# An FFT convolution beside an FFN: other slots for the steps of the convolution and for the last stage of each tile

## The chip, the cores and the metric

The kernel runs on one core of a Trainium2 chip. A core has a matrix engine (TensorE, PE in the profile, with its weight loads listed as PEld), a vector engine (VectorE, DVE), an activation engine (ScalarE, ACT), a general engine (GpSimd, POOL) and a queue engine that mostly issues transfers (SyncE, SP). Each engine works through its own instructions in order and waits on semaphores that the others raise. The metric is the time of one execution on the device in microseconds (us). Time before: a median of 2299.88 us in three runs (2294.12 to 2300.57).

## The reference: what is computed

```python
batch, seq, d_model = (4, 12544, 128)
...
h_filt = (np.maximum(pos_emb @ w1, 0.0) @ w2) * window
u = x * v
L = 2 * S
Uf = np.fft.rfft(u, n=L, axis=1)
Hf = np.fft.rfft(h_filt, n=L, axis=0)
y = np.fft.irfft(Uf * Hf[None, :, :], n=L, axis=1)[:, :S, :]
x = (x * y).reshape(B * S, D)
...
h = np.maximum(np.maximum(x @ w1, x @ w2), x @ w3)
return h @ w_out
```

A long convolution along the sequence, by Fourier transforms, gated by `x`, for four batches of 12,544 positions and 128 channels. Its result goes through a feed-forward network (FFN) whose 768 hidden values are the maximum of three products, all in float32.

## The kernel before

**Stages.** The convolution of batch 0 and the spectrum of the filter are made first. Then the FFN of batch 0 runs with the convolution of batch 1 beside it, the FFN of batch 1 beside the convolution of batch 2, and so on. The FFN of the last batch runs alone, with another arrangement. In this text "batch b" of a schedule is the batch whose convolution is laid out, so it lies beside the FFN of batch b - 1.

**Slots.** The FFN of one batch has `NT` = 32 tiles of 392 positions, and each tile has `NF` = 6 slots, one for each 128 hidden values: 192 slots to a batch. The main loop (from L1100) issues in each slot: `up` (two products into the three `hps` buffers, taken in turn; ScalarE's relu of the first, VectorE's maximum with the second), perhaps sums of the next tile (`t_sums`), `down` of the slot two before (into `ops`, with the extra product `lin` at a tile's first), perhaps the next tile's last stage `t_last`, and then, by `run`, the steps of the convolution that are due in this slot. As each engine runs in order, this order of issue is the order of the work on each engine.

**The last stage of a tile.** `t_load` brings `zt` (what the convolution left in `zd`) and `xT`. `t_sums` makes two sums of 90x512 values, on GpSimd in the first part of a batch and on VectorE later. `t_last` multiplies them by `f4p` into one of two `cps` buffers, and VectorE multiplies the result by `xT` into `gt` (L717), the FFN's input. The `plan` has for each tile the slots of its two sums and of `t_last` (0 to 5).

**The convolution's steps.** They come in two parts.

- *Units*: `NU` = 32 of them. A unit's chain is `u_load` (two loads, SyncE's queue), `u_mul` (VectorE), `u_planes` (GpSimd splits into 16-bit planes), `u_dma` (a transposing transfer, SyncE's queue), `u_join` (ScalarE and VectorE), and `u_first` (32 matmul records into a `cps` buffer, then one copy on ScalarE and two operations on VectorE that write `spec`).
- *Pairs*: `NK` + `LATE` = 48 steps `x`, two to a start slot, called a double here. Each does a `g_quarter` into a `cps` buffer (a first half for pair `x`, a second for pair `x - 3`), and `g_fold` one slot (for odd `x` two slots) later. `w_load`, `q_load` and `h_load` bring its operands over SyncE's queue; `q_swap`, `q_re`, `q_im`, `q_unfold` multiply by the filter's spectrum on ScalarE, VectorE and GpSimd; `g_store` writes `zd` from GpSimd's queue.

`t_last`, `u_first` and `g_quarter` take the two `cps` buffers in turn, one each:

```python
pairs = itertools.cycle([cps.tile([P, 1024], FP32, name=f"cps{i}") for i in range(2)])
```

**The planner.** `conv_steps` (L577) gives each step its slot. `per_pair` is the number of slots per pair; units are 0.6 of it apart. `done` units (6 in batch 1, none later) have been prepared before. `s0` is the slot of the first double and `start(x)` the slot of step `x`. `emptiest` puts sums and VectorE's part of the pairs into the slot with the least planned load. The position `last` of `t_last` in its tile is the first of 3, 4, 2 that is not the slot after a double's start. The slots of one batch's steps begin at 0 and end by 182.

Of the kernel before, what the change touches and what calls it, by code (L numbers as in the profile page):

```python
# [28 lines left out]
LATE = 3  # L29
# [62 lines left out]
def kernel(  # L92
# [16 lines left out]
    NG, _, _, B, NB = x.shape  # L109
# [3 lines left out]
    NF = DFF // P  # L113
    NK = N1 // 2
# [37 lines left out]
    def halves_mm(out, lhsT, rhs, start, stop):  # L152


        for h in range(2):
            nc.tensor.matmul(out[64 * h:64 * h + 64], lhsT[:, 64 * h:64 * h + 64], rhs,  # L156
                             start=start, stop=stop, skip_group_check=True)
# [183 lines left out]
    NU = NG  # L341
# [235 lines left out]
    def conv_steps(b, done):  # L577


        out = []  # L580

        def at(slot, late, fn, *args):
            out.append((slot, late, len(out), fn, args))

        for u in range(4, done):
            at(2 * u - 7, 1, u_first, u)
        per_pair = 170 / (NK + LATE + 0.6 * (NU - done))
        for u in range(done, NU):  # L590
            s = (u - done) * 0.6 * per_pair + 9
            at(max(0, int(s) - 9), 0, u_load, b, u)
            at(int(s) - 6, 0, u_mul, u)
            at(int(s) - 5, 0, u_planes, u)
            at(int(s) - 4, 0, u_dma, u)
            at(int(s), 0, u_join, u)
            at(int(s + 1), 1, u_first, u)
        s0 = int((NU - done - 1) * 0.6 * per_pair + 9) + 6

        def start(x):  # L600
            return s0 + int(x // 2 * 2 * per_pair)

        load = [0.6] * (NT * NF)
        for x in range(NK + LATE):
            s = start(x)
            load[s] -= 1.2
            load[s + 1 + x % 2] += 1.4

        def emptiest(among, cost):
            s = min(among, key=lambda i: load[i])  # L610
            load[s] += cost
            return s

        plan = []
        folds = {start(x) + 1 for x in range(NK + LATE)}
        for i in range(NT - 1):
            s = i * NF
            last = min((3, 4, 2), key=lambda k: s + k in folds)
            load[s + last] += 0.6
            if s <= s0:  # L620
                plan.append((0, 0, last))
                continue
            a = emptiest(range(s, s + 2), 0.7) - s
            plan.append((a, emptiest(range(s + a, s + max(a + 1, last - 1)), 0.7) - s, last))
        plan.append((3, 3, 4))

        for x in range(NK + LATE):
            s, odd = start(x), x % 2
            g, z = x if x < NK else None, x - LATE if x >= LATE else None
            at(s, 1, g_quarter, g, z)  # L630
            at(s + 1 + odd, 0, g_fold, g, z)
            at(s - 4, 0, w_load, x)
            if z is not None:
                at(s + 3 + odd, 0, g_store, b, z)
            if g is None:
                continue
            if g % 2 == 0:
                at(s - 4, 0, q_load, g, min(2, NK - g))
                at(s - 1, 0, h_load, g, min(2, NK - g))
            first = s + 2 + 2 * odd  # L640
            at(first, 0, q_swap, g, 0)
            at(first + 1, 0, q_swap, g, 64)
            last = start(x + LATE) - 1
            a = emptiest(range(first + 1, min(first + 3, last - 1) + 1), 0.7)
            at(a, 0, q_re, g)
            a = emptiest(range(a, min(first + 4, last - 1) + 1), 0.7)
            at(a, 0, q_im, g)
            two = sorted(emptiest(range(a + 1, last + 1), 0.55) for _ in range(2))
            for q in range(2):
                at(two[q], 0, q_unfold, g, q)  # L650
        slots = {}
        for s, _, _, fn, args in sorted(out, key=lambda r: r[:3]):
            slots.setdefault(s, []).append((fn, args))
        return slots, plan, s0


    N = 4 * NB
    NT = P // 4
    zts, xTs, gs, pos_, obs = ({} for _ in range(5))

    def t_load(b, i):
        zt = hp.tile([N1, 2, 512], FP32, tag="zt", name="zt", bufs=2)
        for c in range(2):
            if b == 0:
                nc.sync.dma_start(
                    zt[NK * c:NK * c + NK],
                    zd[b].rearrange("(g a) c t f -> g a c t f", a=2)[
                        :, :, c, 2 * i:2 * i + 2, :].rearrange("g a t f -> g a (t f)"))
                continue
            q, j = divmod(i, NT // 2)  # L670
            for a in range(2):
                nc.sync.dma_start(
                    zt[NK * c:NK * c + NK, a].rearrange("g (t f) -> g t f", t=2),
                    zd[b].rearrange("(g a) c t q f -> g a c t q f", a=2)[
                        :, a, c ^ (a & q), 2 * j:2 * j + 2, q, :])
        zts[b, i] = zt[:, 0], zt[:, 1]
        if i % 2:
            return
        xT = hp.tile([D, 2, 4, NB], FP32, tag="xT", name="xT", bufs=2)
        for c in range(GC):  # L680
            nc.sync.dma_start(xT[c * NG:(c + 1) * NG].rearrange("d i p n -> d (i p) n"),
                              x[:, 4 * i:4 * i + 8, c, b, :])
        xTs[b, i], xTs[b, i + 1] = xT[:, 0], xT[:, 1]
# [3 lines left out]
    def t_sums(i, eng=nc.gpsimd, parts=(0, 1)):  # L687
        z0, z1 = zts[i]
        if 0 in parts:
            evens_[i] = hp.tile([N1, 512], FP32, tag="even", name="even", bufs=2)  # L690
        even = evens_[i]
        for a, (out, op) in enumerate(((even[:], ALU.add), (z1, ALU.subtract))):
            if a not in parts:
                continue
            if i[0] == 0 or i[1] < NT // 2:
                eng.tensor_tensor(out=out, in0=z0, in1=z1, op=op)
            else:
                nc.vector.scalar_tensor_tensor(out=out, in0=z1, scalar=sign_t[:, 0:1], in1=z0,
                                               op0=ALU.mult, op1=op)
        if 1 in parts:  # L700
            zts[i] = evens_.pop(i)[:], z1

    def t_last(i):
# [7 lines left out]
        for s in range(4):  # L711
            for a in range(2):
                halves_mm(y[:, s, a * h:a * h + h], zt[a][:, s * D:(s + 1) * D],
                          f4p[:, i[0] > 0 and i[1] >= NT // 2, a, :], s == 0 and a == 0, True)
        y = y.rearrange("d p (a m) -> d p m a", a=2)
# [124 lines left out]
    def run(steps):  # L840
        for fn, args in steps:
            fn(*args)
# [58 lines left out]
    for f in range(0, FO, 4):  # L901
        quad([hs[:, f + i] for i in range(4)], (f1h[:, 0], f1h[:, 1]), specH[:, :, :, f:f + 4])
        u, k = divmod(f // 4, 4)
# [11 lines left out]
    for u in range(0, NU, 2):  # L915
        t = uts.pop(u)
        for v in range(2):
            if u + 4 < NU:
                u_mul(u + 4 + v)
            at = 4 * (u + v)  # L920
# [94 lines left out]
    EARLY = 6  # L1015
# [80 lines left out]

    tiles = [(b, i) for b in range(B) for i in range(NT)]
    LAST = (B - 1) * NT
    late = []
    for n, (b, i) in enumerate(tiles[:LAST]):  # L1100
        if i == 0:
            beside, plan, pairs_from = conv_steps(b + 1, EARLY if b == 0 else 0)
        if n == 0:
            t_load(*tiles[0])
            t_load(*tiles[1])
            t_sums(tiles[0], nc.vector)
            u_first(2)
            t_last(tiles[0])
            u_first(3)
        for f in range(NF):  # L1110

            if i < NT - 2:
                if f == 0:
                    t_load(*tiles[n + 2])
            elif i == NT - 1 and f < 2 and n + 1 + f < len(tiles):
                t_load(*tiles[n + 1 + f])
            turn_ = i == NT - 1
            if f == 4 and n + 1 == LAST:
                t_sums(tiles[n + 2], nc.vector)
            h = up((b, i), f)  # L1120
            for a in range(2):
                if f == plan[i][a]:
                    t_sums(tiles[n + 1],
                           nc.vector if turn_ or i * NF > pairs_from else nc.gpsimd, (a,))
            late.append(((b, i), f, h))
            if len(late) > 2:
                down(*late.pop(0))
            if f == plan[i][2]:
                t_last(tiles[n + 1])
            if f == 5 and n + 1 == LAST:  # L1130
                t_last(tiles[n + 2])
            s = i * NF + f
            run(beside.pop(s, ()))
            if s == NT * NF - 1:
                assert not beside, sorted(beside)
    first = up((B - 1, 0), 0)
    for l in late:
        down(*l)
# [23 lines left out]
    step, b = 0, B - 1  # L1162
    for i in range(0, NT, 2):
        h = {}
        X, Y = banks if i % 4 == 0 else banks[::-1]
        for j, (name, f) in enumerate(ORDER):
            n = int(name[1]) - 1
# [64 lines left out]
```

## Time and profile before

| what | value |
|---|---|
| the profiled execution's own time | 2298.59 us |
| its span, first to last instruction | 2296.8 us |
| granted TensorE clock, mean | 0.997 |
| median of three runs | 2299.88 us |
| `hps` matmuls (`up`) | 6144 records, 1148.4 us busy |
| `ops` matmuls by `hid` (`down`) | 2304 records, 479.2 us busy |
| `u_first` matmuls (L413) | 3008 records, 134.2 us busy |
| quarter matmuls (L467, L477) | 4320 records, 87.7 and 83.0 us busy |
| `gt` (L717) beside a convolution | 98 operations, 564 ns each |
| unfold (L523) | 270 operations, 594 ns each |
| `ut` loads to landing, median | 4.1 and 4.4 us |
| `sq` loads to landing, median | 7.1 us |

A row of a timeline has the start in us from the span's start, the length in us, the engine (with a q where it is the engine's queue of transfers), the line, the operation, its output and inputs by the program's names, the shape, the number of merged instructions, and in brackets the idle time before it with what ended that. Matmuls are pipelined and their ends are modelled, so the length of a slot is best read from start to start: from the first `hps` row of one slot to that of the next. A row of waits says who waited for whom, for how long in total, how often, and the longest.

### The profile page before, as it was taken

Reading aid. Unit: us, or ns where it says so; the run is one execution under the profiler, and the core shown is the slowest. Engines: PE = TensorE matmul, PEld = TensorE weight load, DVE = VectorE, ACT = ScalarE, POOL = GpSimd, SP = SyncE. Lnnn points to the kernel's source line nnn. Section 1 sums busy time; section 2 is a strip of 40 time slices with the busy share of each in tenths; the row PEclk is TensorE's granted clock in tenths of the full one; section 3 lists DMA queues with packets and bytes.
Section 4 is the critical chain, followed back from the end, with each engine's and each line's share of the span. In section 5 each row is a group of like instructions: output and inputs, shape, how many; then the busy total and the mean of one; then the engine's idle time right before and its main releaser. Section 6 shows DMA issues by size and latency. Waiting matters only on the chain.

```text
span 2296.8 us, 68538 instructions
## 1 busy us (share of the span) xinstructions
PE 2262.9 (99%) x27855; PEld 1375.4 (60%) x27855; DVE 1555.3 (68%) x2848; ACT 1174.7 (51%) x2124; POOL 876.0 (38%) x1093
## 2 busy tenths in 40 slices
PE   8999989999999999999999999999999999999998
PEld 7988866655555546655555546655555556666665
DVE  5588957667878747758887847757887854445443
ACT  2688834456666534446666624446666622222222
POOL 2044423323333234413333324323333326666666
PEclk9999999999999999999999999999999999999999
DMA  7779969799999669969999759969999832222221
GB/s 186 182 235 272 297 159 184 148 212 240 238 232 232 170 142 190 185 149 259 241 238 249 199 126 200 185 147 233 248 253 246 211 90 55 55 64 66 63 55 22
DMA packets 473269, 411.03 MB, mean 179 GB/s; under 512 B 327865, under 2 KB 374426, under 8 KB 472954
## 3 DMA queue, kind: packets, MB, share of 16 engines
q1 hardware_dynamic: 445954, 329.48, 63.9%
q0 software_dynamic: 26288, 75.47, 11.1%
q8 instruction: 219, 3.59, 0.7%
q10 hardware_dynamic: 712, 1.70, 0.3%
q14 instruction: 96, 0.79, 0.1%
HBM read 262.84 MB, written 84.67 MB: 151 GB/s over the span
## 4 chain that ended last, share of the span: by engine, by line
PE 87%; DMA 6%; DVE 3%; SPq 1%; issue 1%; ACT 1%; POOL 0%; DVEq 0%; POOLq 0%; ACTq 0%
PE hps L156 40%; PE ops L156 16%; PE ops L790 6%; PE cps L413 5%; PE cps L156 3%; PE ps L156 3%; PE ps L165 3%; PE cps L467 3%; PE cps L477 2%; DMA ht<-hd 2%; PE sps L1000 2%; PE gps L982 1%; DMA wt<-wq_const 1%; PE last L156 1%; DMA hd<-ht 1%; DMA sq<-spec 1%
## 5 line engine op out<-in xcount | busy, mean ns | idle before, releaser
L156 PE MATMUL hps<-gt,w_sb 128*64 128x392 f32 x6144 | 1148.4, 494 | 0.0
L727 ACT ACTIVATE hid<-hps 128x392 f32<-128x392 f32 x768 | 383.9, 500 | 727.6 <-PE hps L156 712.8
L156 PEld LDWEIGHTS hps<-gt,w_sb 128*64 128x64 f32 x6144 | 427.9, 137 | 423.3 <-issue 395.2
L730 DVE TENSOR_TENSOR hid<-hid,hps 128x392 f32<-128x392 f32 x768 | 428.4, 558 | 342.9 <-PE hps L156 338.0
L156 PE MATMUL ops<-hid,wo_sb 128*64 128x392 f32 x2304 | 479.2, 492 | 0.0
L519 POOL TENSOR_TENSOR cb<-cb,xs 128x512 f32<-128x512 f32 x135 | 174.5, 1292 | 474.3 <-DVE xs L516 347.7
L156 PEld LDWEIGHTS ops<-hid,wo_sb 128*64 128x64 f32 x2304 | 170.2, 137 | 209.0 <-issue 209.0
L424 DVE TENSOR_TENSOR spec<-cps,high 128x360 f32<-128x360 f32 x188 | 141.3, 793 | 127.3 <-ACT high L422 126.3
L492 DVE TENSOR_TENSOR cb<-cps,eo 128x512 f32<-128x512 f32 (+1 forms) x288 | 175.3, 650 | 72.0 <-ACT eo L489 72.0
L745 POOL DMA_DIRECT2D out_dram<-ot x96 | 74.9, 781 | 366.8 <-ACT ot L743 312.6
L507 ACT ACTIVATE xs<-cb 32x512 f32<-32x512 f32 x270 | 169.5, 628 | 19.6 <-DVE cb L492 10.9
L508 ACT COPY xs<-cb 32x512 f32<-32x512 f32 x270 | 166.3, 616 | 3.1
L422 ACT COPY high<-cps 128x360 f32<-128x360 f32 x94 | 75.1, 799 | 162.1 <-PE cps L413 131.6
L523 DVE TENSOR_TENSOR xs<-cb 128x256 f32<-128x256 f32 x270 | 147.9, 594 | 10.9 <-POOL cb L519 10.9
L413 PEld LDWEIGHTS cps<-f1q,uT 98*64 98x64 f32 x3008 | 130.7, 137 | 32.6 <-issue 32.0
L413 PE MATMUL cps<-f1q,uT 98*64 98x90 f32 x3008 | 134.2, 241 | 2.2 <-DVE spec L424 1.5
L382 POOL COPY planes<-ut 128x784 uint16<-128x784 uint16 x90 | 75.7, 841 | 119.4 <-DVE ut L361 117.4
L500 POOL DMA_DIRECT2D zd<-cb x135 | 92.7, 689 | 50.8 <-DVE cb L492 47.6
L156 PEld LDWEIGHTS cps<-f4p,even 90*64 90x64 f32 x1568 | 89.9, 138 | 35.2 <-issue 33.2
L814 POOL DMA_DIRECT2D out_dram<-o x128 | 77.4, 610 | 51.8 <-DVE o L807 49.6
L156 PE MATMUL cps<-f4p,zt 90*64 90x49 f32 x1568 | 97.2, 222 | 0.0
L467 PE MATMUL cps<-sq,wt 64*64 64x128 f32 x2160 | 87.7, 277 | 8.8 <-DVE gt L717 6.9
(134 smaller groups left out, 3149.1 us busy)
## 6 DMA issues: line engine op xcount, KB each, us to landing
ht<-hd SPq DMA_DIRECT2D x264, 256.0 KB, 6.9
wt<-wq_const SPq DMA_DIRECT2D x144, 256.0 KB, 6.3
zd<-cb POOLq DMA_DIRECT2D x135, 256.0 KB, 6.3
zt<-zd SPq DMA_DIRECT2D x384, 90.0 KB, 3.0
sq<-spec SPq DMA_DIRECT2D x264, 128.0 KB, 7.1
ut<-in_xr_dram SPq DMA_DIRECT2D x128, 196.0 KB, 4.1
ut<-in_vr_dram SPq DMA_DIRECT2D x128, 196.0 KB, 4.4
xT<-in_x_dram SPq DMA_DIRECT2D x256, 98.0 KB, 3.7
```

The lines of the kernel that those rows point to most:

```text
L156: nc.tensor.matmul(out[64 * h:64 * h + 64], lhsT[:, 64 * h:64 * h + 64], rhs, start=start, stop=stop, skip_group_check=True)
L413: nc.tensor.matmul(ps[64 * c:64 * c + 64, 256 * i + h * N1:256 * i + (h + 1) * N1], t[:, 2 * ((at + i) % 8) + h].rearrange("n r t -> n (r ...
L424: nc.vector.tensor_tensor(out=spec[:, :, a, at:at + n], in0=v[:, 1], in1=high, op=op)
L467: nc.tensor.matmul(ps[64 * a:64 * a + 64, at:at + D], w[64 * r:64 * r + 64, k, a, :], t[64 * r:64 * r + 64, k, a, :], start=(k == 0), stop ...
L492: nc.vector.tensor_tensor(out=cb[:, a, lo:hi], in0=ps[:, lo:hi], in1=eo[:, lo:hi], op=op)
L507: nc.scalar.mul(xs[at:at + 32], xt[at + 32:at + 64], -1.0)
L508: nc.scalar.copy(xs[at + 32:at + 64], xt[at:at + 32])
L519: nc.gpsimd.tensor_tensor(out=xts[g], in0=xts[g], in1=xs[:], op=ALU.add)
L523: nc.vector.tensor_tensor(out=ab[:, q], in0=y[:, 0], in1=y[:, 1], op=(ALU.subtract, ALU.add)[q])
L727: nc.scalar.activation(h[:], pa[:, 0:N], Relu)
L730: nc.vector.tensor_tensor(out=h[:], in0=h[:], in1=pb[:, 0:N], op=ALU.max)
L790: nc.tensor.matmul(ps[64 * c:64 * c + 64, 0:H2], w, rhs[:, H2 * c:H2 * c + H2], start=start, stop=True, skip_group_check=True)
```

## The change

The planner gets other numbers. The last slot that a double may start in is set to about 177 by `END`; the first unit's join moves from slot 9 to slot 6 in batch 1 and to slot 1 in batches 2 and 3, where the loads and the next steps of the first units get negative slots. These are issued in the last slots of the FFN of the batch ahead; for that the steps of all batches are gathered in one table before the loop. The slots per double are 5.44 (from 5.35) in batch 1 and 5.29 (from 5.06) in batches 2 and 3, and `s0` is 52 (from 55) and 56 (from 62). `last` now avoids a double's start slot first of all, and the slot after it next.

```diff
         for u in range(4, done):
-            at(2 * u - 7, 1, u_first, u)
-        per_pair = 170 / (NK + LATE + 0.6 * (NU - done))
+            at(2 * (u - 4), 1, u_first, u)
+        lead, low = (1, -NT * NF) if b > 1 else (6, 0)
+        share = UNIT * (NU - done - 1)
+        per_pair = (END - lead - 6) / (share + (NK + LATE) // 2 * 2 - 2)
         for u in range(done, NU):
-            s = (u - done) * 0.6 * per_pair + 9
-            at(max(0, int(s) - 9), 0, u_load, b, u)
-            at(int(s) - 6, 0, u_mul, u)
-            at(int(s) - 5, 0, u_planes, u)
-            at(int(s) - 4, 0, u_dma, u)
+            s = (u - done) * UNIT * per_pair + lead
+            load_ = max(low, int(s) - 9)
+            at(load_, 0, u_load, b, u)
+            mul = max(load_ + 2, int(s) - 6)
+            at(mul, 0, u_mul, u)
+            at(max(mul, int(s) - 5), 0, u_planes, u)
+            at(max(mul + 1, int(s) - 4), 0, u_dma, u)
             at(int(s), 0, u_join, u)
             at(int(s + 1), 1, u_first, u)
-        s0 = int((NU - done - 1) * 0.6 * per_pair + 9) + 6
+        s0 = int(share * per_pair + lead) + 6
...
-        folds = {start(x) + 1 for x in range(NK + LATE)}
+        busy = {start(x): 2 for x in range(NK + LATE)}
+        for x in range(NK + LATE):
+            busy.setdefault(start(x) + 1, 1)
         for i in range(NT - 1):
             s = i * NF
-            last = min((3, 4, 2), key=lambda k: s + k in folds)
+            last = min((3, 4, 2), key=lambda k: busy.get(s + k, 0))
...
+    UNIT, END = 0.6, 178
...
+    besides, plans = {}, []
+    for b in range(1, B):
+        slots, *rest = conv_steps(b, EARLY if b == 1 else 0)
+        plans.append(rest)
+        for s, steps in slots.items():
+            besides.setdefault((b - 1) * NT * NF + s, []).extend(steps)
...
-            s = i * NF + f
-            run(beside.pop(s, ()))
+            run(besides.pop(n * NF + f, ()))
```

No step is added or taken away: every engine executes the same instructions, in another order.

More of the change, by code (lines that the diff above doesn't have):

```diff
@@ L1099 @@
     late = []
+    besides, plans = {}, []
[4 more added lines that the diff above has]
+            besides.setdefault((b - 1) * NT * NF + s, []).extend(steps)
     for n, (b, i) in enumerate(tiles[:LAST]):
         if i == 0:
-            beside, plan, pairs_from = conv_steps(b + 1, EARLY if b == 0 else 0)
+            plan, pairs_from = plans[b]
         if n == 0:
@@ L1131 @@
                 t_last(tiles[n + 2])
-            s = i * NF + f
-            run(beside.pop(s, ()))
-            if s == NT * NF - 1:
-                assert not beside, sorted(beside)
+            run(besides.pop(n * NF + f, ()))
+    assert not besides, sorted(besides)
     first = up((B - 1, 0), 0)
```

## The prediction, made before the changed kernel was run

> **What bounds the kernel.** I read the page's first part, then TensorE's waits over the span, then TensorE's timeline around each of those waits, then VectorE's and GpSimd's timelines beside it.
>
> ```profile
> PE 2262.9 (99%) x27855; PEld 1375.4 (60%) x27855; DVE 1555.3 (68%) x2848; ACT 1174.7 (51%) x2124; POOL 876.0 (38%) x1093
> ```
>
> ```profile
> PE cps L467 <- DVE gt L717: 6.9, 8, 0.9
> ...
> PE cps L413 <- DVE spec L424: 1.5, 1, 1.5
> ...
> PE cps L467 <- DMA sq<-spec: 1.1, 2, 0.7
> ...
> PE cps L477 <- DVE gt L717: 0.8, 1, 0.8
> ```
>
> TensorE (PE) is busy 99% of the span. A wait line reads: us in total, times, longest. The largest wait is one thing: a quarter stage (L467, once L477) waits nine times for VectorE (DVE) to finish `gt`, the product that ends a tile's last stage (`t_last`). So TensorE's work sets the end, and a change that only moves work can win what TensorE loses in waits and nothing else. The 2,296.8 us span holds about 1,559 us of FFN slots with a convolution beside them (313.5 to 1872.9).
>
> The length of a slot is the step from one `up` to the next in TensorE's timeline. Undisturbed slots repeat to 0.02 us: bare 1.98; plus 0.66 with `lin`; plus 0.91 with `t_last`; plus 1.24 with a unit's `u_first`; plus 2.05 with a double, two `g_quarter` in one slot (0.05 of it in the slot after). Prices do not depend on the neighbours: `t_last` and a unit in one slot make 4.15, the sum. **So the order of work is free on TensorE unless something waits.** In the unit stage nothing waits:
>
> ```profile
> 850.00:990.00 140.00, 140.00 (x1794) 87.66 (x1792) 97.10 (x172) 65.38 (x113) 55.91 (x78) 1.00 1.04 180
> ```
>
> The columns are the window, its length, busy time of PE, PEld, DVE, ACT, POOL, the clock, DMA share, GB/s. TensorE is busy 140.00 of 140 us at clock 1.00, and every slot there has its plain price. Units wider apart win nothing here.
>
> **What the change removes.** From the old formulas I list where a double starts in the slot of a `t_last`: batch 1 slots 81, 87, 129, 135, 177; batches 2 and 3 slots 87, 117, 153 each. That is eleven. TensorE at slot 81, then at slot 87 of batch 1:
>
> ```profile
> 538.00 1.49 PE L156 MATMUL hps<-gt,w_sb 128*64 128x392 f32 x8
> ...
> 541.48 0.62 PE L477 MATMUL cps<-xs,wt 64*64 64x128 f32 x16
> 542.92 0.67 PE L467 MATMUL cps<-sq,wt 64*64 64x128 f32 x16 [0.83 <-DVE gt L717]
> 543.41 0.62 PE L477 MATMUL cps<-xs,wt 64*64 64x128 f32 x16
> 543.96 1.54 PE L156 MATMUL hps<-gt,w_sb 128*64 128x392 f32 x8
> ```
>
> ```profile
> 554.54 1.49 PE L156 MATMUL hps<-gt,w_sb 128*64 128x392 f32 x8
> ...
> 558.02 0.62 PE L477 MATMUL cps<-xs,wt 64*64 64x128 f32 x16
> 558.46 0.62 PE L467 MATMUL cps<-sq,wt 64*64 64x128 f32 x16
> 558.90 0.62 PE L477 MATMUL cps<-xs,wt 64*64 64x128 f32 x16
> 559.44 1.54 PE L156 MATMUL hps<-gt,w_sb 128*64 128x392 f32 x8
> ```
>
> Slot 81 lasts 5.96 us, slot 87 lasts 4.90 with the same content. There are two `cps` buffers in turn: `t_last` takes one, the first quarter the other, and the second quarter needs the first one back, which `gt` frees. VectorE tells why it is late at 81:
>
> ```profile
> 539.47 2.44 DVE L523 TENSOR_TENSOR xs<-cb 128x256 f32<-128x256 f32 x4
> 541.84 0.55 DVE L730 TENSOR_TENSOR hid<-hid,hps 128x392 f32<-128x392 f32 x1
> 542.31 0.55 DVE L717 TENSOR_TENSOR gt<-cps,xT 128x392 f32<-128x392 f32 x1
> ```
>
> `gt` stands behind four unfolds and a `max`; it ends at 542.87, and the quarter starts at 542.92. At 87 the sums were spread, and `gt` ran at 557.65, in time.
>
> Nine of the eleven stall. Slot lengths: 5.96, 5.96 (81, 129), 5.95, 6.04, 6.03 (batch 2), 5.96, 6.05, 6.04 (batch 3), against 4.90; and 5.07 (177) against 3.12 + 0.91 = 4.03. The excesses sum to 1.06 + 1.06 + 1.05 + 1.14 + 1.13 + 1.06 + 1.15 + 1.14 + 1.04 = **9.8 us**.
>
> A rule weighed: the waits view shows only 6.9 + 0.8 = 7.7 us. The Trainium skill, "TensorE: Matmul & The Clock Gate" (Single matmul latency, and Step-by-step), says that a matmul's drain is normally hidden under the next one and puts the fixed part at 166 ns warm; a wait lays it bare. By it: 7.7 + 9 x 0.166 = 9.2. The start-to-start rows say 9.8, and I take the rows.
>
> The new formulas put no double in a `t_last` slot and no `t_last` in the slot after one (where a fold is due). Tiles' last stages now sit in the slot ahead of a double, two after it, or clear of both. Old slots with `t_last` one ahead (75, 123) have doubles at 4.00 us in the next slot, against 3.98 plain: no stall. At 75, `gt` ran at 526.51 to 527.07, and the second quarter began at 528.40, 1.3 us later. So the 9.8 us go, and what is late next has 1.3 us of slack.
>
> **What it adds.**
>
> *Sums one slot ahead of `t_last`.* Position 2, never chosen before, now appears 13 times: 56, 110, 116, 170, 176 in batch 1; 86, 92, 134, 176 in batches 2 and 3. In nine of them both sums come in slot 1, right before it. From slot 1's start: `max` ends at about 2.05, two sums of 0.69 to 0.90 end by 3.7; `t_last` comes after 1.98 + 2.63 = 4.6. Slack 0.9 us. Behind the sums on VectorE stand two multiplies (0.68 each), then the next `max` and `gt`, now ahead of the unfolds; `gt` ends near 6.2, the double's second quarter needs it near 8.5. Cost: 0; if every place had VectorE a slot behind, 13 x 1.0 = 13.
>
> The second rule, which speaks against this: "SBUF — State Buffer" (Who interferes with whom) says that a VectorE instruction with two SBUF inputs contends with a GpSimd one that reads SBUF, and that the loser waits for the whole instruction. The trace agrees: at slot 81 GpSimd's add (L519) ran 539.32 to 540.63, and the first unfold took 1.4 us where the least is 0.41. A sum held for a whole add (1.29) would pass the slack by 0.4, so by the rule up to 9 x 0.4 = 3.6 us. But GpSimd's add of a pair follows its multiply `q_im`, which in these tiles is queued behind the sums in the same slot; the add before it is three slots old. I take 0, and keep 3.6.
>
> *Unit chains at a batch's start.* In batch 1 units 4 and 5 go to slots 0 and 2 (from 1 and 3), the next three load in slot 0, and two multiplies come in slot 2 instead of 3 and later. SyncE issued these loads back to back already (314.65 to 320.7); they landed at 320.2 and 321.5. The `max` of slot 2 ends near 319.9, so VectorE would be held until 322.1, then has a unit's two subtractions (1.5 us): the `max` of slot 3 ends at 324.2 instead of 323.2. Its `hps` buffer is needed by slot 5, at 326.2. Cost 0; without that cover 1.7.
>
> *Batches 2 and 3, last slots of the FFN ahead.* Unit loads in slots 184 to 191, multiplies from 187, GpSimd's planes from 188, SyncE's transposes from 189. SyncE's queue there was empty from 785.4 to 809.67, where it waited for `zd` to land before loading `zt`. The first two units' loads (four DMAs, about 0.5 us each) fall in that hole, ahead of the `zt` load; the DMA share was 0.33 in 800 to 830, and VectorE was busy 12.16 of 30 us. Transposes wait for planes; behind them stands a `zt` load needed a tile later. GpSimd gets two planes (1.2 us each) ahead of the next tile's sums (2.6), which are due three slots later. Cost 0, at most 2 us at each of two boundaries. The distances inside a unit's chain stay as they were.
>
> *Pairs.* They start at 56 instead of 62 and go 5.29 slots per double instead of 5.06 (batch 1: 52, 5.44 for 5.35), so VectorE has more room; one more tile's sums per batch go from GpSimd to VectorE, which that room hides. The second double after the start waited for `sq` (slot 67: 5.17 and 4.42 against 3.55, so 1.6 and 0.9 us): SyncE issued `sq` at 1011.59 behind 18 other DMAs. In batches 2 and 3 all that surrounds it moves by exactly one tile, so it stays; it could go (-2.5). A unit's late join cost 0.6 at slot 24; it may go or return (-0.6 to +0.6).
>
> **Sum.** The profiled execution took 2298.59 us (1.8 around its span), 1.3 under the median 2299.88 of three. 2298.59 - 9.8 = 2288.8; from the median 2290.1. I forecast **2290**.
>
> **Rivals.**
> 1. *Everything else waits less too* (wider pairs): also -2.5 - 0.6 -> 2287. Against: the `sq` order is unchanged. Chance 0.12.
> 2. *The stall follows `gt`*: held unfolds and sums keep VectorE a slot behind, the double one slot later still waits in about half of the places: -5 -> 2295. For: VectorE is busy 221 of 280 us in this stage; against: 4.00 us at 75 and 123. Chance 0.16.
> 3. *Slower*: the 13 sums right ahead of `t_last`. If VectorE is a slot behind there, TensorE waits for them. It decides from 9.8 / 13 = 0.75 us per place; at 1.3 us, +17 - 9.8 -> 2307. Against: the 0.9 us of slack. Chance 0.10.
> The forecast has 0.62, its own range 2286 to 2294.
>
> **Numbers.** The three runs before spread over 6.5 us, 0.3%, which is about what this measurement tells from no change. Faster by over that means under 2293: nearly all of the forecast and rival 1, 0.70. Within: rival 2, the forecast's upper end, part of rival 3: 0.21. Slower: 0.09. Range 2284 (rival 1 and a run at the low end) to 2298 (rival 2 and the start costs).
>
> **What would show it.** TensorE's waits for `gt` gone (7.7 to under 1 us); every double at 3.98 to 4.00; slots 184 to 191 longer only by their own work; VectorE's waits for `ut` loads near 316 to 322; `last` of 2 without a TensorE wait on L696 or L698. Wrong: new waits of L156 on `even` or `zt`, or of L413 on `uT`, or doubles still at 6.

## The result and the profile after

The changed kernel takes a median of 2287.69 us (2285.93 to 2289.95, six runs). The kernel before has 2299.32 (2294.12 to 2302.31, six runs). The ratio is 0.9953, with a 95% interval of 0.994 to 0.9966. So it is faster by 11.6 us, where 9.8 were forecast; by the interval the gain lies between 7.8 and 13.8 us, so the medians can't tell the one from the other. The profiled execution took 2287.75 us with a span of 2285.9, which is 10.9 less than before, at a mean clock of 0.996.

The busy times and, from the chain that ended last, the shares by engine, on the page of the kernel after:

```profile
PE 2259.9 (99%) x27855; PEld 1382.0 (60%) x27855; DVE 1557.4 (68%) x2854; ACT 1174.3 (51%) x2124; POOL 873.0 (38%) x1087
...
PE 95%; DVE 2%; DMA 1%; issue 1%; ACT 0%; POOL 0%; SPq 0%; POOLq 0%; DVEq 0%; ACTq 0%
```

TensorE's busy time is 3.0 us less, for the same matmuls; the rest of the gain is idle time. VectorE has six operations more and GpSimd six fewer (one more tile's two sums in each of three batches), so the engines' instructions are not quite the same as before. In the chain of before, TensorE had 87% and transfers 6%.

TensorE's waits in the kernel after that belong to a `cps` buffer, out of the waits view:

```profile
PE cps L413 <- DVE spec L424: 1.7, 1, 1.7
...
PE cps L413 <- DVE uT L397: 1.1, 3, 0.4
...
PE cps L413 <- ACT lin L1080: 0.4, 1, 0.4
```

The view has no wait of a quarter stage (L467, L477) any more, neither for `gt` nor for `sq`. The first and third rows stand at the start of the first FFN in both kernels. The middle row has grown. One tile of batch 1, where `t_last` and a double had shared slot 81, on TensorE's timeline of the kernel after:

```profile
535.05 1.49 PE L156 MATMUL hps<-gt,w_sb 128*64 128x392 f32 x8
...
537.12 0.67 PE L467 MATMUL cps<-sq,wt 64*64 64x128 f32 x16
537.61 0.62 PE L477 MATMUL cps<-xs,wt 64*64 64x128 f32 x16
538.05 0.62 PE L467 MATMUL cps<-sq,wt 64*64 64x128 f32 x16
538.49 0.62 PE L477 MATMUL cps<-xs,wt 64*64 64x128 f32 x16
539.03 1.54 PE L156 MATMUL hps<-gt,w_sb 128*64 128x392 f32 x8
```

The double now has slot 79 to itself. Its four groups follow one another without a gap, and the slot lasts 539.03 - 535.05 = 3.98 us. `t_last` runs in slot 81.

**Where the time went.** For every slot of the three FFN stages with a convolution I took its length less the plain price of its content, and kept what is over 0.15 us:

| excess over the plain price, us | before | after |
|---|---|---|
| a double with `t_last` in its slot | 9.8 (9 places) | 0 |
| a double alone, waiting for its operands | 3.9 (4 places) | 0.2 (1) |
| `u_first`, waiting for `uT` | 0.6 (1) | 2.1 (4) |
| slot 0 of batch 1, at a low granted clock | 0 | 1.7 |

That is -9.8 - 3.6 (3.88 less 0.24) + 1.5 + 1.7 = -10.2 us; from the first slot to the last of these stages the kernel went from 1559.32 to 1549.09 us. The other 0.7 came ahead of the first slot, which started at 312.89 instead of 313.54. The last FFN took what it did before, to 0.2 us.

### The profile page after: what moved, and what is told of

Read it like the earlier page. It is cut to its first block, busy times and chain, and to the rows that moved or that the text cites. A ratio compares the mean times of both kernels' runs of the same rounds, so it can differ in the third digit from the quotient of the medians.

```text
span 2285.9 us, 68499 instructions
## 1 busy us (share of the span) xinstructions
PE 2259.9 (99%) x27855; PEld 1382.0 (60%) x27855; DVE 1557.4 (68%) x2854; ACT 1174.3 (51%) x2124; POOL 873.0 (38%) x1087
## 4 chain that ended last, share of the span: by engine, by line
PE 95%; DVE 2%; DMA 1%; issue 1%; ACT 0%; POOL 0%; SPq 0%; POOLq 0%; DVEq 0%; ACTq 0%
PE hps L156 44%; PE ops L156 19%; PE ops L797 6%; PE cps L413 5%; PE cps L156 4%; PE cps L467 3%; PE ps L156 3%; PE ps L165 3%; PE cps L477 3%; PE sps L1007 2%; PE gps L989 1%; PE last L156 1%; PE pst L366 1%; DMA hd<-ht 1%; PE pm L328 1%
## 5 line engine op out<-in xcount | busy, mean ns | idle before, releaser
L156 PEld LDWEIGHTS hps<-gt,w_sb 128*64 128x64 f32 x6144 | 432.7, 137 | 419.5 <-issue 393.8
L492 DVE TENSOR_TENSOR cb<-cps,eo 128x512 f32<-128x512 f32 (+1 forms) x288 | 175.1, 649 | 74.0 <-ACT eo L489 74.0
L523 DVE TENSOR_TENSOR xs<-cb 128x256 f32<-128x256 f32 x270 | 139.9, 562 | 10.3 <-POOL cb L519 10.1
L382 POOL COPY planes<-ut 128x784 uint16<-128x784 uint16 x90 | 76.6, 851 | 150.9 <-DVE ut L361 150.9
L156 PE MATMUL cps<-f4p,even 90*64 90x49 f32 x1568 | 96.1, 220 | 0.0
```

Source lines behind the costliest of these rows:

```text
L492: nc.vector.tensor_tensor(out=cb[:, a, lo:hi], in0=ps[:, lo:hi], in1=eo[:, lo:hi], op=op)
L523: nc.vector.tensor_tensor(out=ab[:, q], in0=y[:, 0], in1=y[:, 1], op=(ALU.subtract, ALU.add)[q])
```

## The experiments

In each diff "before" or "after" says which kernel it edits. Excess has the meaning of the table.

### The rule for `t_last` alone, the slots alone, and the rule turned round

Before, with the new rule for `last` and nothing else:

```diff
-        folds = {start(x) + 1 for x in range(NK + LATE)}
+        busy = {start(x): 2 for x in range(NK + LATE)}
+        for x in range(NK + LATE):
+            busy.setdefault(start(x) + 1, 1)
-            last = min((3, 4, 2), key=lambda k: s + k in folds)
+            last = min((3, 4, 2), key=lambda k: busy.get(s + k, 0))
```

> Before with nothing but the new rule for the position of t_last (never in a double's start slot); units, pairs and their spacing as before. Theory A (the nine waits of doubles for gt are what that rule is worth): TensorE's waits for gt (L717) fall from 7.7 us to under 1, the slots that lasted 5.95 to 6.05 us last 4.0, and the time falls by 9.8 us, a ratio of 0.9957. The waits for sq that before had (1.6, 0.9, 1.0 us in slots 67, 67 and 102) stay. Theory B (wider pairs give VectorE the room that removes the waits, the rule alone only moves them one slot on): waits for gt stay above 4 us and the ratio is 0.998 or more.

After, with the old rule for `last`, so with the new slots alone:

```diff
-            last = min((3, 4, 2), key=lambda k: busy.get(s + k, 0))
+            last = min((3, 4, 2), key=lambda k: s + k in folds)
```

> After with the old rule for the position of t_last; the new slots of units and pairs stay. By the formulas 13 doubles now share their slot with a t_last (batch 1: 57, 111, 117, 171, 177; batches 2 and 3: 87, 93, 135, 177 each). Theory A: 10 or 11 of them wait, about 1.06 us each, waits for gt of 8 to 9 us in the trace; waits for sq near 0; the time is within 3 us of before, ratio 0.998 to 1.001. Theory B (wider pairs are the gain): waits for gt under 4 us, ratio 0.9965 or less.

After, with the rule turned round, so that `t_last` seeks a double's slot:

```diff
-            last = min((3, 4, 2), key=lambda k: busy.get(s + k, 0))
+            last = min((3, 4, 2), key=lambda k: (0, 2, -1)[busy.get(s + k, 0)])
```

> After with the rule for t_last turned round: it is put into a double's start slot wherever one of the positions 3, 4, 2 is one (14 tiles in batch 1, 12 each in batches 2 and 3: 38 in all, against none in after and 11 in before). A dose of the suspected cost. Theory A (gt is late behind VectorE's queue and holds the second quarter): three quarters or more wait, about 1.05 us each, so 28 to 38 us more than after; TensorE's waits for gt (L717) of 22 to 32 us in the trace; ratio to before 1.007 to 1.012. Theory B (what counts is the spacing, the shared slot is an accident): under 10 us more than after, ratio under 1.000.

| kernel | median us (range) | ratio to before, 95% | shared slots that wait, their excess |
|---|---|---|---|
| rule alone | 2288.18 (2287.47 to 2289.03) | 0.9965 [0.9951, 0.9979] | 0 |
| slots alone | 2295.3 (2292.82 to 2297.83) | 0.9996 [0.9987, 1.0005] | 10 of 13, 9.4 us |
| rule turned round | 2315.87 (2313.69 to 2317.08) | 1.0087 [1.0073, 1.0101] | 27 of 38, 30.2 us |

The waits view says what the quarters wait for. In the kernel with the rule alone, it is operands only:

```profile
PE cps L467 <- DMA wt<-wq_const: 2.0, 3, 1.0
```

In the kernel with the slots alone it is `gt`, as before (the line numbers are those of each kernel):

```profile
PE cps L467 <- DVE gt L722: 4.5, 6, 0.9
...
PE cps L477 <- DVE gt L722: 2.4, 3, 0.8
```

And in the kernel with the rule turned round:

```profile
PE cps L467 <- DVE gt L724: 16.7, 18, 1.2
PE cps L477 <- DVE gt L724: 4.8, 5, 1.2
```

The rule alone takes every `gt` wait away and is worth 8.8 us; the slots alone leave them (in other places; 6.9 us in the view, where 8 to 9 were expected) and are worth 1.6, not told from nothing. Turned round, the excess trebles, and the kernel becomes slower than before. So the stall belongs to a double in the slot of `t_last`, and wider spacing doesn't cure it. Whether the new slots add anything to the rule isn't shown by the times, as the intervals of the rule alone and of the whole change overlap; in the profiled executions the FFN stages with a convolution take 1550.88 and 1549.09 us.

The expectation for the turned rule was not exact: 27 of 38 is less than three quarters, and the places don't all wait alike. Three of them are a batch's first double (slots 52, 56, 56), where nothing stands ahead of `gt` on VectorE, and they lose 0.32 us each: that much the shared slot costs without a long job. Others wait longer than the 1.05 us expected. VectorE at such a place, slot 82 of batch 2, in the kernel with the rule turned round:

```profile
1065.68 0.68 DVE L703 TENSOR_TENSOR zt<-zt 90x512 f32<-90x512 f32 x1
1066.28 0.68 DVE L511 TENSOR_TENSOR cb<-cb,ht 128x512 f32<-128x512 f32 x1
1066.88 0.68 DVE L516 TENSOR_TENSOR xs<-xs,ht 128x512 f32<-128x512 f32 x1
1067.48 0.55 DVE L737 TENSOR_TENSOR hid<-hid,hps 128x392 f32<-128x392 f32 x1
1067.95 2.50 DVE L523 TENSOR_TENSOR xs<-cb 128x256 f32<-128x256 f32 x4
1070.38 0.55 DVE L737 TENSOR_TENSOR hid<-hid,hps 128x392 f32<-128x392 f32 x1
1070.85 0.55 DVE L724 TENSOR_TENSOR gt<-cps,xT 128x392 f32<-128x392 f32 x1
```

A sum, two multiplies and a maximum stand ahead of the four unfolds, which begin 1.97 us into the slot (it starts at 1065.98). In the kernel with the slots alone the same row of work at slot 87, with `t_last` at position 3, lies half a microsecond earlier, with the unfolds from 1.47 us. So `gt` comes later here, and the slot has 1.61 us too many instead of 1.06.

### Position 2 throughout

After, with 2 the first position tried, so that 71 tiles have it instead of 13:

```diff
-            last = min((3, 4, 2), key=lambda k: busy.get(s + k, 0))
+            last = min((2, 3, 4), key=lambda k: busy.get(s + k, 0))
```

> After with position 2 tried first for t_last, then 3, then 4: 71 tiles instead of 13 have t_last in slot 2, the sums in slots 0 and 1 right ahead of it. A dose of what my rival 3 took for the danger. My sum (0.9 us of slack between the end of the sums and t_last): no wait of TensorE for even or zt at L156, the time within 1.5 us of after, ratio to before 0.994 to 0.997. Rival 3 (TensorE waits for the sums, 0.5 us or more per place): 58 more places, at least 29 us, ratio over 1.005.

Measured: 2289.82 us (2287.37 to 2291.22), ratio 0.9971 [0.9961, 0.9981]. The waits view has one row for a sum:

```profile
PE cps L156 <- DVE zt L703: 0.2, 1, 0.2
```

It stands at 310.09 us, ahead of the first slot. In the loop there is none; one slot (164 of batch 1) is 0.14 us over its price. The FFN stages are 2.4 us longer than in the kernel after; 2.0 us are quarters that wait for their operands, in five slots (the kernel after has 0.2).

The dose is smaller than it looks. By the plan, 27 of the 58 added tiles lie in the unit stage, where GpSimd makes the sums, and 27 have VectorE's sums in slot 0, a slot further ahead. Only four more have both in slot 1 (13 for nine). At the 1.3 us per place of the slower rival, the 31 with VectorE's sums would still cost 40 us against the kernel after; it is refuted. But the slack of 0.9 us is not what kept the cost at 0. VectorE and then TensorE in the kernel after, around slot 110 of batch 1 (slot 109 starts at 614.62):

```profile
616.03 1.29 DVE L492 TENSOR_TENSOR cb<-cps,eo 128x512 f32<-128x512 f32 x2 [1.22 <-ACT eo L489]
617.23 0.55 DVE L737 TENSOR_TENSOR hid<-hid,hps 128x392 f32<-128x392 f32 x1
617.70 0.68 DVE L703 TENSOR_TENSOR even<-zt 90x512 f32<-90x512 f32 x1
618.42 0.69 DVE L703 TENSOR_TENSOR zt<-zt 90x512 f32<-90x512 f32 x1
...
619.23 0.27 PE L156 MATMUL cps<-f4p,even 90*64 90x49 f32 x4
```

Two folds (L492), held by ScalarE's copy `eo`, stand ahead of the maximum, which ends 3.16 us after the start of slot 109. The second sum ends 0.12 us before `t_last` starts. Of the nine places with both sums in slot 1, six have a slack of 0.12 us or none and three have 0.74 to 0.81.

### Why the second double no longer waits

In the kernel before, the second double of batches 2 and 3 waited for its operands (slot 67). Two kernels ask whether that hangs on the spacing or on the tile that it falls into. The first is the kernel after with the pairs of batches 2 and 3 at the old 5.06 slots per double, first double at 56 (the units too go back to the old spacing, so everything lies six slots ahead of where it was):

```diff
-        lead, low = (1, -NT * NF) if b > 1 else (6, 0)
+        lead, low, END = (3, -NT * NF, 172.4) if b > 1 else (6, 0, 178)
```

> After, but in batches 2 and 3 the pairs have before's spacing (5.06 slots per double) and the first double is in slot 56, so every double is exactly six slots, one tile, ahead of before. Tests why the wait for sq at the second double went, which I had said would stay. Theory C (xT is loaded only with every other tile; a shift by one tile takes its four loads out of the queue ahead of sq): no wait for sq at the second double (slot 61 lasts 3.55 us in both batches), while the late waits of batch 3 that belong to the narrow spacing (about 0.4 to 1.0 us at two doubles) can come back, in all up to 1.5 us. Theory D (the wider spacing alone did it): slot 61 lasts 4.4 to 5.2 us, waits for sq of 1 us or more in the trace. Time: C 2287 to 2290, D 2289 to 2291; the trace tells them apart.

The second is the rule alone (old slots), but `xT` for two tiles is brought with the odd tile ahead of them:

```diff
-        if i % 2:
+        if b < B - 1:
+            if i and (i % 2 == 0 or i == NT - 1):
+                return
+            i += i % 2
+        elif i % 2:
```

> The kernel of e1 (before with the new rule for t_last), with one more edit: for the first three batches a tile pair's xT is loaded with the odd tile ahead of the pair instead of with its even tile. No slot of the convolution is moved. Theory C (the four xT loads in front of sq in the queue are what made the second double late): the waits at the second double go (slot 67 of batches 2 and 3 lasts 3.55 us instead of 5.02 and 4.05), and the time falls by 1.5 to 3 us against e1, ratio to before 0.995 to 0.996. Theory D (the narrow spacing makes it late): slot 67 still lasts over 4 us in both; ratio as e1's, 0.9965.

With the old spacing, the second double (slot 61) has its plain price in both batches; the kernel takes 2288.28 us (2284.47 to 2288.87), ratio 0.9963 [0.9949, 0.9976], with 0.9 us of other waits at doubles of batch 2 (slots 76 and 96). With `xT` moved in the old slots, slot 67 is plain in both batches, while the rule alone keeps 1.47 and 0.50 us there. A new wait of 1.05 came at the third double of batch 3. Its time of 2287.72 (2285.04 to 2290.88), ratio 0.9967 [0.9953, 0.998], can't be told from that of the rule alone.

SyncE's rows of the timeline ahead of the second `sq` of batch 2, in the kernel before:

```profile
1000.59 2.48 SPq L438 DMA_DIRECT2D sq<-spec  x4
1003.11 0.59 SPq L428 DMA_DIRECT2D wt<-wq_const  x1
1003.81 1.74 SPq L672 DMA_DIRECT2D zt<-zd  x4
1005.60 1.87 SPq L681 DMA_DIRECT2D xT<-in_x_dram  x4
1007.82 3.25 SPq L451 DMA_DIRECT2D ht<-hd  x4
1011.12 0.43 SPq L428 DMA_DIRECT2D wt<-wq_const  x1
1011.59 1.78 SPq L438 DMA_DIRECT2D sq<-spec  x2
```

The same rows in the kernel after:

```profile
986.33 2.49 SPq L438 DMA_DIRECT2D sq<-spec  x4
988.87 0.58 SPq L428 DMA_DIRECT2D wt<-wq_const  x1
989.56 1.75 SPq L679 DMA_DIRECT2D zt<-zd  x4
991.36 1.81 SPq L451 DMA_DIRECT2D ht<-hd  x4
993.21 0.43 SPq L428 DMA_DIRECT2D wt<-wq_const  x1
993.70 3.23 SPq L438 DMA_DIRECT2D sq<-spec  x4
...
1002.70 1.15 SPq L688 DMA_DIRECT2D xT<-in_x_dram  x2
```

From the first `sq` to the second the queue took 11.0 us before and takes 7.4 now. `xT` comes only with even tiles. The double moved by one tile, so the four `xT` loads are no longer ahead of `sq`. They are 2.2 of the 3.6 us (1005.60 to 1007.82). The rest is the `ht` row, 3.25 us for the same four transfers that take 1.81 after; the cause of that is open, and batch 3 of the kernel before doesn't have it: 1.91 us there, and 9.4 from `sq` to `sq`. The second `sq` now lands 2.3 and 2.5 us before it is used in the two batches. By moving the transfer in the old slots, and by keeping the old spacing in the new ones, the two kernels put this on the tile's parity and not on the spacing. Batch 3's old waits at slots 77 and 102 went too. With the rule alone slot 77 is plain already, while slot 102 keeps 1.11 us and is plain once `xT` is moved as well; each of these is one execution, and neither was tried apart.

### Why four units wait now

A theory for the new `uT` waits: where a unit's `u_first` falls into slot 0 of a tile, GpSimd may be making the next tile's sums while VectorE copies `uT` for it. So in the kernel after, the sums in all such slots go to VectorE:

```diff
-                           nc.vector if turn_ or i * NF > pairs_from else nc.gpsimd, (a,))
+                           nc.vector if turn_ or i * NF > pairs_from or i and any(
+                               fn is u_first for fn, _ in besides.get(n * NF + f, ()))
+                           else nc.gpsimd, (a,))
```

> After, but where a unit's u_first comes in a tile's slot 0 in the unit stage, that tile's two sums run on VectorE instead of GpSimd. Theory E (the four new waits of u_first for uT, 0.3 to 0.6 us each, come from the join's copy on VectorE being held while GpSimd makes the sums: 1.36 us instead of 0.45): TensorE's waits for uT vanish, the copies L397 take 0.45 us in those slots, and the four slots of 3.55 to 3.82 us last 3.22; the time falls by 2.1 us against after, ratio to before about 0.9944. Theory F (the join is late because its transfer or the queue of VectorE is late): the waits stay or grow, since VectorE gets 1.4 us more per such tile; ratio 0.995 to 0.996.

The four `uT` waits are gone, and slots 18, 36 and 24 are plain: 2285.7 us (2283.77 to 2287.32), ratio 0.9955 [0.9941, 0.9968]. The timeline of the kernel after around its slot 18:

```profile
364.02 1.28 POOL L703 TENSOR_TENSOR even<-zt 90x512 f32<-90x512 f32 x1
...
365.37 1.27 POOL L703 TENSOR_TENSOR zt<-zt 90x512 f32<-90x512 f32 x1
...
365.83 1.36 DVE L397 COPY uT<-turned 98x512 uint16<-98x512 uint16 x1
...
367.34 1.46 PE L413 MATMUL cps<-f1q,uT 98*64 98x90 f32 x32 [0.38 <-DVE uT L397]
```

And VectorE's timeline in the same place with those sums moved to it:

```profile
367.55 0.46 DVE L397 COPY uT<-turned 98x512 uint16<-98x512 uint16 x1
...
368.84 1.06 DVE L703 TENSOR_TENSOR even<-zt 90x512 f32<-90x512 f32 x1
369.93 0.69 DVE L703 TENSOR_TENSOR zt<-zt 90x512 f32<-90x512 f32 x1
```

The copy takes 1.36 us beside GpSimd's sum and 0.46 without it; TensorE waits for it in the one case and not in the other. That `u_first` falls into slot 0 isn't enough. In the kernel after it does so beside sums in 14 slots (18, 24, 36 and 42 in batch 1; 6, 24, 30, 36 and 48 in batches 2 and 3), and only four wait. In eight of the others the copy begins about 0.9 us before the slot and is done in time; in slot 48 no sum runs beside it. In the four, it begins 1.0 us into the slot, with GpSimd's second sum still running.

### The start of batch 1, and three kernels on one chip

The kernel of the last experiment (after, with those sums moved), with the first tile's `t_last` issued ahead of `u_first` of units 2 and 3 before the first slot:

```diff
-            u_first(2)
...
+            u_first(2)
```

> The kernel of e5, with one more edit: ahead of the first slot of batch 1 the order is t_last, u_first(2), u_first(3) instead of u_first(2), t_last, u_first(3). Meant as a better version. Theory: u_first(3) no longer waits 1.65 us for a cps buffer that u_first(2)'s two VectorE operations free, while TensorE still waits for zt first; the first slot starts 0.4 us sooner, gt is ready sooner, and if the idle gap was also what lowered the granted clock in the next 4 us, 1 to 2 us more. Time 0.4 to 2.4 us under e5, ratio to before 0.9945 to 0.9955. Rival: the start waits for zt and then for gt either way, so it is worth nothing, within 0.5 us of e5.

Measured 2284.54 us (2284.25 to 2290.59), ratio 0.9957 [0.9944, 0.997]. The wait for `spec` is gone, and a wait of 1.1 us for `lin` stands in its place. Slot 0 starts at 312.48 us, against 314.34 without the reordering. Three kernels were then run once more beside each other: the kernel after, the one with the sums moved, and the one with the start reordered as well.

> After itself, beside e5 and e8 on the same chip, since all were timed against before alone. Ratio to before 0.9945 to 0.996. In the trace: no wait for gt, up to five waits of u_first for uT (1.5 to 2.3 us of slot time), and the first slot of batch 1 slowed if the granted clock is low there (0.6 to 2 us, by chance).

> The kernel of e5 beside after. If the slots tell the whole time, 2.1 us under after (the four uT waits), with no wait for uT in the trace; if the two sums on VectorE cost something elsewhere, the same as after within 1 us.

> The kernel of e8 beside after. If the slots tell the whole time, 2.1 to 4 us under after. Rival: the start is bound by zt and by lin and its order is worth nothing, so it is equal to e5 within 0.5 us.

| kernel | median us (range) | ratio to before, 95% | FFN stages, us | slot 0 starts at |
|---|---|---|---|---|
| after | 2287.41 (2285.52 to 2288.15) | 0.995 [0.9937, 0.9962] | 1549.04 | 310.70 |
| sums moved | 2286.31 (2284.78 to 2287.31) | 0.9946 [0.9932, 0.9959] | 1545.62 | 314.91 |
| and start reordered | 2285.53 (2285.29 to 2290.7) | 0.9949 [0.9937, 0.9962] | 1545.99 | 318.84 |

The FFN stages of the kernel with the sums moved are 3.4 us shorter: 2.3 from the `uT` waits, 1.1 from a smaller loss of clock in slot 0. That the whole kernel is faster than the one after isn't shown: the intervals overlap, and the start of slot 0, ahead of which the first two kernels do the same work, lies between 310.7 and 318.8 us in the profiled executions of this study. The low clock of the slots around it is a part of that. The reordered start brings nothing that shows: slot 0 came 1.9 us sooner with it in the first pair of profiled executions and 3.9 us later in the second.

## Why the prediction was right, and where its steps were off

- **TensorE's waits for `gt`: right.** The nine stalls were the largest part, and their size, 9.8 us from start to start, is what the table gives. The weighing of 7.7 in the waits view against 9.8 in the rows came out for the rows, slot by slot; the 8.8 us of the rule alone by median can't tell the estimate of 9.2 from 9.8. "Doubles at 3.98 to 4.00" holds but for one slot (98 of batch 3, 0.24 over).
- **"What is late next has 1.3 us of slack": right.** The tightest double of the kernel after has 1.33 us between the end of `gt` and its second quarter. Rival 2, the stall that follows `gt` into the next slot, didn't come in any place.
- **Sums one slot ahead of `t_last`: right at 0, but by luck.** TensorE waits in none of the 13 places, and rival 3 is refuted. The reason given, a slack of 0.9 us, was wrong: it had the maximum of slot 1 end 2.05 us into that slot and left out the two folds ahead of it. At slot 109 it ends at 3.16, and in six of nine places 0.12 us or nothing is left. The rule of the Trainium skill's "SBUF — State Buffer" (Who interferes with whom), priced at up to 3.6 us for these sums, cost nothing, and was not put to the test: as argued, no add of GpSimd ran beside any of them, and they took 0.68 to 0.75 us each.
- **"All that surrounds it moves by exactly one tile, so it stays": wrong.** This is the step that failed. A shift by one tile is not neutral, because `xT` is loaded with every second one. The second double's waits were worth 1.6 and 0.9 us, as the prediction had them, and both went. I also missed slots 77 and 102 of batch 3 (0.4 and 1.0 us). That the total still came near 9.8 is in part luck: 3.6 us were won at these doubles and 3.2 lost again to `uT` and the clock, and with 0.7 ahead of slot 0 the profiled executions differ by 10.9.
- **"A unit's late join may go or return (-0.6 to +0.6)": mis-sized.** It came four times, 2.1 us in place of 0.6, so +1.5. The cause is VectorE's copy held by GpSimd's sum, in two slots of batch 1 and one of each later batch. The list of slots from the formulas was made for the doubles and not for the units; it would have shown where `u_first` meets a tile's slot 0, but not which of these places wait.
- **Unit chains at the start of batch 1: cost 0, by another way.** VectorE was never held by the `ut` loads, so that sign did not appear: its multiplies of `ut` (L361) ran from 320.58 with no wait. What slot 0 lost is clock, and the rule alone, with the old unit slots, lost 1.3 us there too.
- **The last slots of the FFN ahead: right at 0.** Slots 184 to 191 have 1.97 to 1.99 us bare, 2.63 with `lin` and 2.89 with `t_last`.
- **Rival 1 (all waits less, 2287) came nearer than the forecast**, with 0.12 on it: the quarters' operand waits went as it said, the join did not.

## What to carry to other kernels

Where two stages take turns at two buffers, don't issue the second user's pair of steps behind the first user's last one if another engine has to free the buffer behind a long job: shift one of them by a slot, and price the stall from start to start of the slots. When a schedule moves, work through the period of everything around it (every second tile, every sixth slot) before calling it unchanged. A change that works in slots of two microseconds is best judged slot by slot, as the start of this kernel alone varies by more than most of the steps are worth.

## What the runs showed of the hardware that was not expected

**A copy held by GpSimd.** VectorE's copy of `uT` has one input, of 16-bit values. In the kernel after, 62 of its 90 executions take 0.44 to 0.49 us. The other 28 take 0.72 to 1.37 us, and each began while GpSimd was at work: 24 beside the split into planes (L382, 0.84 us), four beside a sum. They end 0.31 to 0.33 us after that operation, or, in nine cases, after the short fill of `planes` (L381, 0.30 us) that GpSimd ran right behind it. So one copy can be held through two of GpSimd's operations. Only the four beside sums came late enough in the slot for TensorE to wait. The section of the Trainium skill that the prediction weighed ("SBUF — State Buffer", Who interferes with whom) names copies in a two-port mode beside the instructions with two SBUF inputs; whether this copy ran in such a mode no run here shows.

**The granted clock at the start of the FFN.** The window 313 to 317 us of the kernel after, its last columns being the clock, DMA share and GB/s:

```profile
313.00:317.00 4.00, 4.00 (x40) 2.60 (x37) 2.03 (x3) 1.29 (x2) 0.97 (x2) 0.57 0.73 172
```

The same window of the kernel before:

```profile
313.00:317.00 4.00, 4.00 (x58) 2.75 (x55) 2.40 (x4) 1.66 (x3) 1.50 (x2) 1.00 0.91 204
```

TensorE is busy all four microseconds in both, but gets 40 records done at a clock of 0.57 and 58 at 1.00. Just ahead of it TensorE had waited 1.65 us for `spec` in the one and 1.45 in the other. A dip of some depth there is in every other profiled execution of this study, with the old unit slots (the rule alone) as well as with the new ones, and costs up to 2 us in slot 0. In the clock's record, the kernel after is at 0.50 from 313.03 to 316.44 us. All 13 profiled executions have an earlier stretch at 0.50 (before from 296.60 to 306.84, after from 295.96 to 306.20), and 12 have a second one around slot 0; each of these stretches lasts 3.41 us or two or three times that. The kernel before is the one without the second. Of it one execution was profiled, so whether it has the dip in others isn't known, and what decides it was not found: two other executions had the dip after a wait for `spec` of 1.37 us, shorter than the 1.45 here.
